# TensorE's loop waits on one semaphore per engine, takes its counts off behind output projections, and transposed x stays in SBUF for the second 16 heads

## Chip, cores, metric

One core of one Trainium2 chip. The metric is the device time of the whole program in microseconds, the median of several runs. Time before: 792.89 us (3 runs, 792.17 to 793.03).

## The reference

Two independent attention blocks, A and B, joined along the last axis. Each has its own x, key cache, value cache and weights, all bf16.

```python
B, Sq, D = 16, 64, 640;  H, Sk, Dh = 32, 512, 128
q = (x @ wq).reshape(B, Sq, H, Dh).transpose(0, 2, 1, 3)
scores = einsum("bhqd,bhkd->bhqk", q, k_cache) * (Dh ** -0.5)
p = softmax(scores)
o = einsum("bhqk,bhkd->bhqd", p, v_cache)
out = o.transpose(0, 2, 1, 3).reshape(B, Sq, H * Dh) @ wo
```

Keys and values are 268 MB of the 298 MB that move. They are read once. The inputs are small, so the scores are close to zero and the softmax is nearly flat.

## The kernel before

The work is cut into 128 *slots* (four heads of one pair of batches) and four *quarters* of 32 slots (16 heads of one block). Each engine has a program of operations sorted by planned time. A slot on TensorE: scores S, transposes of normalized probabilities TR (two halves), output projection OP of an earlier slot, query projection QP of the next slot, weighted sum PV of the slot before. Every fourth slot also transposes x (XT). The other engines and the DMA queue are fully unrolled; TensorE runs a loop of four slots. Its waits must then have the same counts in every turn, so at the end of each turn TensorE subtracts from each semaphore what the turn has consumed.

```python
own = {"XE", "QE", "KT", "NM", "TE", "OE", "OA", "OV", "LDV", "LDX"}   # waited for by TensorE
...
return (("q_" if for_pe(op) else "s_") + op.kind.lower(),)   # one semaphore per kind of operation
...
lo = next(i for i, o in enumerate(pe) if o.kind == "S" and o.idx == cfg.FIRST)   # FIRST = 3, PERIOD = 4
...
for op in prog[:lo]:
    emit(e, op, p, {})
with e.Fori(0, reps):                                        # L720; reps = 31
    for op in prog[lo:lo + size]:
        emit(e, op, p, {})
    for s, v in sorted(per.items(), key=str):
        e.sem_inc(sems[p][s], -v * units(s))                 # L724: the subtractions
```

Loads are issued by SyncE in one fixed order, into rings: 7 slots of K, 4 slots of V, 4 pieces of query weights. Each quarter has 5.2 MB of weights of its own.

```python
# K: rows of 4096 bytes; V: rows of 2048; query weights: rows of 1024; output weights and x: rows of 1280
src = blocks[...][3].rearrange("(kt p) n -> p kt n", p=128)[:, :, c * 512:(c + 1) * 512]
ins = e.dma_start(ws_ring[:, op.idx % NWS], src)             # query weights, four pieces a quarter
...
ins = e.dma_start(xn_ring[:, op.idx % NXN, :], src)          # x, loaded again in every quarter
```

## Time and profile before

| | before |
|---|---|
| time, median | 792.89 us |
| span of the profiled run | 790.7 us |
| TensorE busy | 706.0 us (89%) |
| bytes moved | 297.8 MB |
| starts of S in one turn of the loop | 5.70, 5.41, 5.41, 6.77 us apart |

First the page of the kernel before: TensorE's busy time; then, over 40 equal slices, DMA's busy share in tenths and its rate; the packets; and the engines' shares of the chain that ended last.

```profile
PE 706.0 (89%) x17953; PEld 533.3 (67%) x18081; DVE 616.3 (78%) x1062; ACT 406.8 (51%) x1185; POOL 386.8 (49%) x550
...
DMA  9999999999999999999999999999999999999950
GB/s 319 388 396 397 396 393 396 393 394 384 396 385 397 391 377 393 390 388 370 382 392 393 398 397 397 398 396 390 383 389 387 396 399 397 400 398 399 399 215 15
DMA packets 132396, 297.76 MB, mean 377 GB/s; under 512 B 9472, under 2 KB 34048, under 8 KB 132352
...
PE 60%; PEld 14%; issue 10%; DVE 8%; SPq 4%; DMA 1%; PEldq 1%; ACT 0%; DVEq 0%
```

DMA is at nine tenths or more for almost the whole run, yet the chain is TensorE's: 60% matmuls, 14% weight loads, 10% issue. Two limits lie close together.

TensorE's instructions in order of time around one turn's end (start, duration, engine, line, operation, count, and in brackets the idle time before and what ended it):

```profile
396.83 0.89 PE L622 MATMUL ps<-pT_ring,v_ring 64*128 64x64 bf16 x50
397.66 0.62 PE L604 MATMUL ps<-ident,pn_ring 128*128 128x128 bf16 x8
399.58 0.68 PE L562 MATMUL ps<-kt_ring,qs_ring 32*64 32x512 bf16 x16 [1.30 <-PEq L724]
```

The transposes end at 398.28; S starts at 399.58, after 1.30 us. The line of the subtractions, with what waited for it (us in all, times):

```profile
L724 PEldq EVENT_SEMAPHORE  x372: 51/51/51, 71.2 to 771.8; - x186
...
  PE ps L562: 39.9, 31
```

In the trace they are 12 a turn, 151 ns apart, followed by an add (36 ns) and a compare-and-branch (208 ns): 2.17 us of TensorE's sequencer, from 397.38 to 399.58. About 0.87 us of it lies under the weighted sum and the transposes, which went on meanwhile; 1.30 us shows, 31 times.

The issuing queue's longest wait (us in all, times, longest):

```profile
SPq L508 <- PE ps L622: 243.3, 91, 4.5
```

SyncE waits for V buffers that PV (L622) frees. Last, busy time by stretches of 23.3 us: busy us and (count) of five engines, granted clock, DMA share, GB/s.

```profile
core 0: us, PE busy (x) PEld busy (x) DVE busy (x) ACT busy (x) POOL busy (x), PEclk, DMA share, GB/s
...
263.10:286.40 23.30, 21.78 (x564) 16.51 (x567) 19.13 (x35) 12.65 (x38) 10.85 (x17) 1.00 1.03 377
...
356.34:379.60 23.26, 21.74 (x564) 16.47 (x566) 19.11 (x34) 12.61 (x38) 10.85 (x16) 1.00 1.02 367
...
566.13:589.40 23.27, 21.78 (x564) 16.49 (x567) 19.18 (x34) 12.66 (x39) 18.04 (x23) 1.00 1.05 387
589.44:612.70 23.26, 21.77 (x565) 16.48 (x567) 19.17 (x34) 12.65 (x39) 13.21 (x19) 1.00 1.05 387
612.75:636.10 23.35, 21.83 (x565) 16.55 (x567) 19.28 (x34) 12.70 (x39) 10.91 (x17) 1.00 1.04 399
```

DMA's rate is 367 to 399 GB/s. (A DMA share over 1, here 1.02 to 1.05, means that the packets' times overlap a little.)

### The profile page before, as it was taken

The numbers are of one execution on the slowest core, as the hardware profiler recorded it, in microseconds if no ns is written. First come the engines' busy times: TensorE is split into PE (matmuls) and PEld (weight loads), VectorE is DVE, ScalarE is ACT, GpSimd is POOL, SyncE is SP. The second block draws the span as 40 slices with busy tenths as digits, with TensorE's granted clock in tenths as the row PEclk, the third lists the DMA queues.
The fourth block names the chain that finished last, engine by engine and source line by source line (L and its number), as shares of the span: only waits on it lengthen the run. The fifth ranks groups of instructions, "written<-read, shape, count | busy, mean of one in ns | idle before, by whom it ended". The sixth has DMA issues, their size and how long they took to land.

```text
span 790.7 us, 40216 instructions
## 1 busy us (share of the span) xinstructions
PE 706.0 (89%) x17953; PEld 533.3 (67%) x18081; DVE 616.3 (78%) x1062; ACT 406.8 (51%) x1185; POOL 386.8 (49%) x550
## 2 busy tenths in 40 slices
PE   4668999999999999999999999999999999999994
PEld 3446676776777767767776676767767777677672
DVE  3537888778888788788878888887888887888883
ACT  2334555555546555555555555555555555555551
POOL 5323454444864444445674444444484544444451
PEclk9879999999999999999999999999999999999999
DMA  9999999999999999999999999999999999999950
GB/s 319 388 396 397 396 393 396 393 394 384 396 385 397 391 377 393 390 388 370 382 392 393 398 397 397 398 396 390 383 389 387 396 399 397 400 398 399 399 215 15
DMA packets 132396, 297.76 MB, mean 377 GB/s; under 512 B 9472, under 2 KB 34048, under 8 KB 132352
## 3 DMA queue, kind: packets, MB, share of 16 engines
q1 hardware_dynamic: 130048, 294.69, 98.9%
q10 hardware_dynamic: 2304, 2.62, 0.9%
q8 instruction: 11, 0.18, 0.1%
q14 instruction: 33, 0.27, 0.1%
HBM read 294.65 MB, written 2.62 MB: 376 GB/s over the span
## 4 chain that ended last, share of the span: by engine, by line
PE 60%; PEld 14%; issue 10%; DVE 8%; SPq 4%; DMA 1%; PEldq 1%; ACT 0%; DVEq 0%
PE ps L562 13%; PE ps L604 12%; PE ps L539 11%; PE ps L622 11%; PE ps L638 8%; PE ps L641 5%; PEld ps L539 5%; PEld ps L622 4%; PEld ps L604 3%; DVE pT_ring L610 3%; SPq L501 2%; DVE kt_ring L552 2%; PE ps L522 2%; DMA xn_ring<-in_A_x_dram 1%; PEld ps L638 1%
## 5 line engine op out<-in xcount | busy, mean ns | idle before, releaser
L597 POOL TENSOR_SCALAR pn_ring<-p_ring,recip 128x512 bf16<-128x512 bf16 x512 | 347.7, 692 | 383.1 <-DVE recip L592 382.1
L577 ACT ACTIVATE p_ring<-ps 128x512 bf16<-128x512 f32 x512 | 298.9, 599 | 189.2 <-PE ps L562 189.2
L552 DVE STREAM_TRANSPOSE kt_ring<-kn_ring 128x1024 f32<-128x1024 f32 x256 | 316.4, 1236 | 16.1 <-DMA kn_ring<-in_A_k_cache_dram 15.8
L610 DVE COPY pT_ring<-ps 128x1024 bf16<-128x1024 bf16 x256 | 173.2, 677 | 118.4 <-PE ps L604 117.8
L562 PE MATMUL ps<-kt_ring,qs_ring 32*64 32x512 bf16 x4096 | 147.1, 398 | 46.5 <-PEq L724 39.9
L539 PE MATMUL ps<-xT_ring,wqp_sb 128*128 128x128 bf16 x2560 | 166.3, 221 | 2.4 <-POOL wqp_sb L516 1.3
L539 PEld LDWEIGHTS ps<-xT_ring,wqp_sb 128*128 128x128 bf16 x2560 | 152.5, 114 | 18.7 <-ACT p_ring L577 2.2
L629 ACT ACTIVATE oT_ring<-ps 128x512 bf16<-128x512 f32 x128 | 76.4, 597 | 170.5 <-PE ps L622 170.5
L604 PE MATMUL ps<-ident,pn_ring 128*128 128x128 bf16 x2048 | 159.8, 221 | 1.3 <-DVE pT_ring L610 1.3
L604 PEld LDWEIGHTS ps<-ident,pn_ring 128*128 128x128 bf16 x2048 | 117.3, 98 | 50.5 <-DVE pT_ring L610 42.6
L622 PE MATMUL ps<-pT_ring,v_ring 64*128 64x64 bf16 x8192 | 142.3, 190 | 2.9 <-issue 2.2
L622 PEld LDWEIGHTS ps<-pT_ring,v_ring 64*128 64x128 bf16 x8192 | 126.8, 95 | 15.1 <-issue 2.5
L641 PE MATMUL ps<-wo_sb,oT_ring 128*128 128x128 bf16 x512 | 112.5, 220 | 8.0 <-ACT oT_ring L629 0.9
L638 PE MATMUL ps<-wo_sb,oT_ring 128*128 128x512 bf16 x384 | 118.8, 381 | 0.0
L562 PEld LDWEIGHTS ps<-kt_ring,qs_ring 32*64 32x64 bf16 x4096 | 54.8, 104 | 88.9 <-PEq L724 45.3
L577 ACT ACTIVATION_READ_ACCUMULATOR p_ring<-ps 128x1 f32 x512 | 106.9, 209 | 0.0
L545 DVE TENSOR_SCALAR qs_ring<-ps 128x512 bf16<-128x512 f32 x128 | 85.3, 667 | 0.5 <-PE ps L539 0.5
L638 PEld LDWEIGHTS ps<-wo_sb,oT_ring 128*128 128x128 bf16 x512 | 50.4, 98 | 46.7 <-issue 1.1
L641 PEld LDWEIGHTS ps<-wo_sb,oT_ring 128*128 128x128 bf16 x512 | 50.4, 98 | 0.0
L592 DVE RECIPROCAL recip<-rowsum 128x2 f32<-128x2 f32 x256 | 37.0, 144 | 13.7 <-ACT p_ring L577 13.5
L651 DVE TENSOR_TENSOR acc<-acc,ps 128x128 f32<-128x128 f32 x96 | 27.0, 281 | 10.9 <-PE ps L641 2.1
L528 ACT ACTIVATE xT_ring<-ps 128x640 bf16<-128x640 bf16 x32 | 22.3, 696 | 15.0 <-PE ps L522 15.0
(23 smaller groups left out, 99.7 us busy)
## 6 DMA issues: line engine op xcount, KB each, us to landing
kn_ring<-in_A_k_cache_dram SPq DMA_DIRECT2D x128, 512.0 KB, 9.3
v_ring<-in_A_v_cache_dram SPq DMA_DIRECT2D x128, 512.0 KB, 7.5
kn_ring<-in_B_k_cache_dram SPq DMA_DIRECT2D x128, 512.0 KB, 12.3
v_ring<-in_B_v_cache_dram SPq DMA_DIRECT2D x128, 512.0 KB, 10.5
ws_ring<-in_A_wq_dram SPq DMA_DIRECT2D x8, 640.0 KB, 10.0
wo_sb<-in_A_wo_dram SPq DMA_DIRECT2D x8, 640.0 KB, 10.1
ws_ring<-in_B_wq_dram SPq DMA_DIRECT2D x8, 640.0 KB, 10.4
wo_sb<-in_B_wo_dram SPq DMA_DIRECT2D x8, 640.0 KB, 12.3
```

What stands on the lines that cost most here:

```text
L539: last = e.matmul(ps[:, 0, f * 128:(f + 1) * 128], w[:, kt, f, :], xT_ring[:, xs, kt, :], start=(kt == 0), stop=(kt == KT - 1))
L545: ins = e.tensor_scalar(qs_ring[:, op.idx % NQ].rearrange("p f b q -> p (f b q)"), ps[:, 0, :], scale, None, ALU.mult)
L552: ins = e.transpose(dst, kn_ring[:, n % NK, b, :].bitcast(F32))
L562: last = e.matmul(ps[64 * b:64 * b + 64, i, :], qs_ring[rows, n % NQ, f, b, :], kt_ring[rows, n % NKT, b, :, f // 2, :, f % 2], start=(f = ...
L577: ins = e.activation(dst, src, ACTF.Exp, scale=1.0, accum_out=rowsum[:, h:h + 1])
L597: ins = e.tensor_scalar(pn_ring[:, (h // 2) % NPN, :, h % 2, :], p_ring[:, (h // 2) % NP, :, h % 2, :], recip[:, (h // 2) % NR, h % 2:h % ...
L604: last = e.transpose(pt_ps[:, t, :], pn_ring[:, op.idx % NPN, t].rearrange("q s k -> q (s k)"), ident[:, :])
L610: ins = e.tensor_copy(pT_ring[:, op.idx % NT].rearrange("p t q -> p (t q)"), pt_flat)
L622: last = e.matmul(o_ps[:, s, col:col + 64], v_ring[rows, n % NV, b, a, t, :], pT_ring[rows, (2 * n + a) % NT, t, 64 * b:64 * b + 64], star ...
L629: ins = e.activation(oT_ring[:, op.idx % NO].rearrange("p s a q -> p s (a q)"), o_ps, ACTF.Copy)
L638: last = e.matmul(out_ps0, oT, wo_sb[:, 4 * j + h4, 0:N0], start=(j == 0 and h4 == 0), stop=(j == NJ - 1 and h4 == 3))
L641: last = e.matmul(out_ps1, oT, wo_sb[:, 4 * j + h4, N0:D], start=(h4 == 0), stop=(h4 == 3))
```

## The change

Its intent: take TensorE's loop overhead off the critical path, and load x once per block.

- All operations of one engine that TensorE waits for count on one semaphore. Waits on V keep four. 12 subtractions a turn become 7.
- Each subtraction goes behind an output projection after the last wait on its semaphore; the turn is cut before QP, so the branch lies behind a projection too.
- Transposed x is copied by GpSimd into SBUF (XS) in a block's first quarter and read from there in the second. x's landing is awaited by a ScalarE operation before the x transposes, no longer by TensorE itself. The x transposes on TensorE stay (the loop must be periodic); only their result is not used.
- One K buffer less makes room. The planned times change a little.

```diff
-    NK = 7
+    NK = 6
-    FIRST = 3
+    FIRST = 4
...
+        first = dims["FIRST"](g // NBP)
+        add("act", "XE", g, n0 + AT["XE"], [] if first else [("xs", g % NBP)], [("OB",), ("xT", g % cfg.NX)])
+        if first:
+            add("pool", "XS", g, n0 + AT["XS"], [("xT", g % cfg.NX)], [("xs", g % NBP)])
+            op = add("sp", "LDX", g, txt - 0.5, [], [("xn", g % cfg.NXN)])
...
-    lo = next(i for i, o in enumerate(pe) if o.kind == "S" and o.idx == cfg.FIRST)
+    lo = next(i for i, o in enumerate(pe) if o.kind == "QP" and o.idx == cfg.FIRST)
...
-        return (("q_" if for_pe(op) else "s_") + op.kind.lower(),)
+        return ("q_" + op.eng,) if for_pe(op) else ("s_" + op.kind.lower(),)
...
+def place_takes(turn, per):
+    spots = [i for i, o in enumerate(turn) if o.kind == "OP"] + [len(turn) - 1]
+    load = {i: 0 for i in spots}
+    take = {}
+    for s in sorted(per, key=str):
+        final = max(i for i, o in enumerate(turn) for s2, _ in o.waits if s2 == s)
+        best = min((i for i in spots if i >= final), key=lambda i: (load[i] + 2 * (i == len(turn) - 1), i))
+        load[best] += 1
+        take[s] = best
+    return take
...
-                for s, v in sorted(per.items(), key=str):
-                    e.sem_inc(sems[p][s], -v * units(s))
+                    for s, v in sorted(per.items(), key=str):
+                        if loop["take"][s] == i:
+                            e.sem_inc(sems[p][s], -v * units(s))
+                            taken[s] = v
```

More of the change, by code (lines that the diff above doesn't have):

```diff
@@ L31 @@
     PERIOD = 4
-    FIRST = 3
+    FIRST = 4
     SLOT_US = 5.6
-    AT = dict(XT=-0.999, XE=-0.813, QP=-0.735, QE=-0.179, KT=(-0.798, -0.573), S=0, EX=(0.133, 0.239, 0.393, 0.529),
-              RC=(0.25, 0.562), NM=(0.632, 0.647, 0.673, 0.713), TR=(0.953, 1.086), TE=(1.035, 1.243), PV=1.274,
-              OE=1.62, OP=2.212, OA=2.264, OV=2.887, ST=3.562, WP0=-1.75, WP1=-2.894)
+    AT = dict(XT=-0.998, XE=-0.828, XS=1.064, QP=-0.639, QE=-0.339, KT=(-1.008, -0.378), S=0,
+              EX=(0.14, 0.192, 0.454, 0.611), RC=(0.31, 0.63), NM=(0.476, 0.739, 0.793, 0.91), TR=(0.854, 1.001),
+              TE=(0.983, 1.034), PV=1.464, OE=1.653, OP=2.236, OA=2.301, OV=2.96, ST=3.466, WP0=-1.75, WP1=-2.974)
     DMA_US = dict(LDK=1.27, LDV=1.35, LDWQ=1.75, LDWO=1.75, LDX=0.45)
@@ L84, in build_plan @@
         add("pe", "XT", g, txt, [("xn", g % cfg.NXN), ("ident",)], [("OB",)])
-        add("act", "XE", g, n0 + AT["XE"], [], [("OB",), ("xT", g % cfg.NX)])
-        op = add("sp", "LDX", g, txt - 0.5, [], [("xn", g % cfg.NXN)])
-        loads.append((txt - 0.1, (g - cfg.NXN) * NJ + AT["XT"] if g >= cfg.NXN else -99.0, 0, op))
+        first = dims["FIRST"](g // NBP)
[3 more added lines that the diff above has]
+            op = add("sp", "LDX", g, txt - 0.5, [], [("xn", g % cfg.NXN)])
+            loads.append((txt - 0.1, (g - cfg.NXN) * NJ + AT["XT"] if g >= cfg.NXN else -99.0, 0, op))
     for ph in range(NPH):
@@ L189, in build_plan @@
     pe = progs["pe"]
-    lo = next(i for i, o in enumerate(pe) if o.kind == "S" and o.idx == cfg.FIRST)
-    hi = next(i for i, o in enumerate(pe) if o.kind == "S" and o.idx == cfg.FIRST + cfg.PERIOD)
+    lo = next(i for i, o in enumerate(pe) if o.kind == "QP" and o.idx == cfg.FIRST)
+    hi = next(i for i, o in enumerate(pe) if o.kind == "QP" and o.idx == cfg.FIRST + cfg.PERIOD)
     size = hi - lo
@@ L205, in build_plan @@
             op.deps = [d for d in op.deps if d.kind != "LDWO"]
+        if op.kind == "XT" and op.idx > 0:
+            next(d for d in op.deps if d.kind == "OE").deps.extend(d for d in op.deps if d.kind == "LDX")
+            op.deps = [d for d in op.deps if d.kind != "LDX"]
         if op.kind == "QP" and op.idx > 0:
@@ L208, in build_plan @@
             op.deps = [d for d in op.deps if d.kind != "WP"]
-    own = {"XE", "QE", "KT", "NM", "TE", "OE", "OA", "OV", "LDV", "LDX"}
+    own = {"XE", "QE", "KT", "NM", "TE", "OE", "OA", "OV", "LDV"}
     def for_pe(d):
@@ L268, in build_plan @@
     loop["per"] = per
+    loop["take"] = place_takes(progs["pe"][lo:lo + size], per)
     return progs, counts, loop
+def place_takes(turn, per):
[8 more added lines that the diff above has]
+    return take
 def run_order(progs, visit):
@@ L415, in mha_kernel @@
     for general in (False, True):
-        dims = dict(NPH=NPH, NBP=NBP, NJ=NJ, FINAL=lambda ph: ph % NSUB == NSUB - 1)
+        dims = dict(NPH=NPH, NBP=NBP, NJ=NJ, FIRST=lambda ph: ph % NSUB == 0,
+                    FINAL=lambda ph: ph % NSUB == NSUB - 1)
         plans.append(build_plan(dims, cfg, general))
@@ L433, in mha_kernel @@
         xT_ring = sb("xT_ring", [128, NX, KT, 128], BF16)
+        xs_sb = sb("xs_sb", [128, NBP, KT * 128], BF16)
         xn_ring = sb("xn_ring", [128, NXN, D], BF16)
@@ L527, in em_XE, with em_XS @@
         def em_XE(e, op):
-            ins = e.activation(xT_ring[:, op.idx % NX].rearrange("p k q -> p (k q)"), x_ps[:, 0:KT * 128], ACTF.Copy)
+            src = xs_sb[:, op.idx % NBP, :] if op.idx // NBP % NSUB else x_ps[:, 0:KT * 128]
+            ins = e.activation(xT_ring[:, op.idx % NX].rearrange("p k q -> p (k q)"), src, ACTF.Copy)
+            return ins, ins
+        def em_XS(e, op):
+            ins = e.tensor_copy(xs_sb[:, op.idx % NBP, :], xT_ring[:, op.idx % NX].rearrange("p k q -> p (k q)"))
             return ins, ins
@@ L720, in run_program @@
             with e.Fori(0, reps):
-                for op in prog[lo:lo + size]:
-                    emit(e, op, p, {})
-                for s, v in sorted(per.items(), key=str):
-                    e.sem_inc(sems[p][s], -v * units(s))
+                taken = {}
+                for i, op in enumerate(prog[lo:lo + size]):
+                    emit(e, op, p, taken)
+                    for s, v in sorted(per.items(), key=str):
+                        if loop["take"][s] == i:
+                            e.sem_inc(sems[p][s], -v * units(s))
+                            taken[s] = v
             taken = {s: v * reps for s, v in per.items()}
```

## The prediction

> **What bounds the kernel now.** Two almost equal limits, in a loop of 31 turns of four slots (a slot: four heads of two batches).
>
> TensorE: starts of the score matmuls (instructions in time order) are 5.70, 5.41, 5.41 and 6.77 us apart, 23.3 us a turn. 5.41 us is dense matmul work; 5.70 has the x transposes. 6.77 is the turn's end: 12 semaphore subtractions 151 ns apart (1.81 us), then add and branch (0.36 us). They start before the weighted sum's last matmuls and outlast the transposes behind them; the score matmul then idles 1.30 us (waits view: 39.9 us in 31 times).
>
> DMA: 297.8 MB, share 1.03 to 1.05 in nearly every turn (busy time by stretches). The best sustained rate is 398 GB/s (612 to 752 us); it fell to 377 and 367 GB/s in turns where K and V alone come at TensorE's pace and the issuing queue waits for V buffers (243 us in its waits). A quarter (one block's 16 heads) needs 73.7 MB, 185 us at 398 GB/s; TensorE needs 8 x 23.3 = 186 us.
>
> **What the change does.**
> - One semaphore per engine: I count 7 subtractions a turn (three engines, four V buffers), one or two behind each output projection, and the branch behind one too. A projection streams for 1.09 us, so 0.15 to 0.5 us of sequencer time should fit beneath it. [...]the present subtractions start while the weighted sum still runs. I expect turns of 22.0 to 22.3 us, 34 to 40 us less over 31 turns if nothing else bound.
> - x is loaded once per block: 16 loads of 160 KB less, 2.6 MB, 6.6 us at 398 GB/s. The x transposes remain (0.39 us a turn); ScalarE then copies from SBUF instead of PSUM (0.70 us now). GpSimd copies 16 times, estimated 0.7 us each from its 1.25 us for 1280 columns; it is 49% busy.
> - K buffers 7 to 6: harmless once DMA is the limit. The engines' order stays nearly the same.
>
> **How much counts.** TensorE alone would end near 758 us. But it would ask for 9.1 MB per 22.2 us, over 409 GB/s, which the trace never shows; DMA becomes the limit. 295.1 MB at 396 to 398 GB/s, with the slow first 10 us (253 GB/s), lets the last V land at 746 to 750 us (765 now, held back by V buffers). After it come three more weighted sums at TensorE's pace and the end, 17 to 20 us (now 10 us from the last weighted sum). Span 764 to 769, plus 2 us to the measured time. So about 25 of the 34 to 40 us count; the rest becomes waiting for K and V.
>
> **Predicted: 768 us, 759 to 777 (8 in 10).** Chances: faster by over 2% 0.88, within 2% 0.11, slower 0.01.
>
> **What would show it.** No idle time put down to subtractions; no 6.77 us slots; TensorE waiting for K transposes or V instead; DMA at 395 to 399 GB/s in all turns; V-buffer waits of the issuing queue well under 243 us; 295.1 MB; the first 50 us as slow as now (DMA's).
>
> **What would make it wrong.** Subtractions stalling the queue behind the projections after all (then about 780); merged semaphores or the new order creating waits on VectorE (78% busy); DMA over 400 GB/s once more loads are queued (then near 760); six K buffers starving a quarter's start, where 5.2 MB of weights come on top.

## The result, and the profile after

779.62 us (4 runs, 779.26 to 780.16) against 792.66 us: ratio 0.9836, interval 0.9819 to 0.9853, so 1.6% faster. A ratio is the mean time of one kernel's runs over that of the other's of the same rounds, so it is not quite the ratio of the quoted medians. The prediction had 768 us, 759 to 777, and gave 0.88 to a gain of over 2%. It missed on both counts.

The page of the changed kernel:

```profile
PE 708.3 (91%) x17953; PEld 534.6 (69%) x18081; DVE 607.9 (78%) x1062; ACT 412.2 (53%) x1185; POOL 394.6 (51%) x566
...
DMA  8999999999999999999999999999999999999960
GB/s 318 389 395 397 394 396 395 394 396 391 392 387 399 398 400 400 400 394 394 387 389 395 397 397 397 397 397 398 374 387 388 398 398 399 400 398 400 400 254 15
DMA packets 130096, 295.20 MB, mean 380 GB/s; under 512 B 9216, under 2 KB 31744, under 8 KB 130048
...
PE 54%; SPq 27%; DMA 14%; issue 2%; DVE 2%; ACT 0%; DVEq 0%; ACTq 0%
SPq L531 13%; PE ps L567 11%; PE ps L590 11%; SPq L524 11%; PE ps L632 11%; PE ps L650 11%; PE ps L666 7%; DMA kn_ring<-in_B_k_cache_dram 6%; DMA v_ring<-in_A_v_cache_dram 5%; PE ps L669 4%; DMA kn_ring<-in_A_k_cache_dram 2%; SPq L517 2%; D
```

The chain has turned: TensorE's 74% (60% matmuls and 14% weight loads) are 54%, its issue went from 10% to 2%, and 41% are now the DMA queue and landings (SPq 27%, DMA 14%). TensorE at a turn's end, in a stretch that nothing holds:

```profile
481.38 0.62 PE L632 MATMUL ps<-ident,pn_ring 128*128 128x128 bf16 x8
481.84 0.44 PE L545 MATMUL ps<-ident,xn_ring 128*128 128x128 bf16 x5
...
483.15 0.22 PE L669 MATMUL ps<-wo_sb,oT_ring 128*128 128x128 bf16 x1
483.20 1.28 PE L567 MATMUL ps<-xT_ring,wqp_sb 128*128 128x128 bf16 x20
```

No line has idle time in brackets: transposes, x transposes, projection and QP follow each other. The subtractions' line, now L754, has nobody waiting for it (no line follows "who waited" in this view):

```profile
L754 PEldq EVENT_SEMAPHORE  x210: 51/51/51, 53.6 to 735.4; - x105
...
who waited for it (us, times):
```

7 a turn, in 30 turns. The trace has the last four and the branch from 481.58 to 482.49, while TensorE works on transposes and projection until 483.2. The issuing queue's wait for V buffers fell from 243.3 us to:

```profile
SPq L531 <- PE ps L650: 48.8, 30, 3.8
```

What TensorE waits for instead is K (its transposes on VectorE, and the scaled q that VectorE can only give after them):

```profile
DVE kt_ring L580 <- DMA kn_ring<-in_B_k_cache_dram: 24.6, 16, 3.6
PE ps L590 <- DVE qs_ring L573: 23.7, 15, 3.2
DVE kt_ring L580 <- DMA kn_ring<-in_A_k_cache_dram: 16.1, 5, 7.3
```

The same stretches as before:

```profile
263.10:286.40 23.30, 23.09 (x617) 17.68 (x621) 20.16 (x36) 13.51 (x38) 12.14 (x19) 1.00 1.04 399
...
356.34:379.60 23.26, 21.80 (x564) 16.49 (x566) 18.82 (x34) 12.86 (x38) 15.49 (x21) 1.00 1.05 388
...
566.13:589.40 23.27, 18.85 (x506) 14.40 (x506) 14.28 (x25) 10.40 (x31) 14.29 (x18) 1.00 1.05 388
589.44:612.70 23.26, 16.84 (x424) 12.46 (x425) 15.70 (x28) 10.00 (x29) 8.22 (x13) 1.00 1.04 393
612.75:636.10 23.35, 22.72 (x593) 16.98 (x597) 20.25 (x36) 12.91 (x37) 12.02 (x18) 1.00 1.04 399
```

In the first one TensorE is busy for 23.09 of 23.30 us. Around the start of the last quarter (566 to 613 us) it is busy for 18.85 and 16.84 us, and the third quarter's start looks alike (20.52 and 17.95 us in two such stretches from 380 to 426 us), although DMA's share is full (1.04 and 1.05 in all four). TensorE got its time back and waits there for data.

Starts of S, and the end of the span, show where the time went (worked out from the starts in the traces, us):

```
                S4     S104    S127    end    | S4 to S104  S104 to end
before         53.1   638.1   772.2   790.7  |   585.1        152.6
changed        52.5   629.7   758.2   777.3  |   577.2        147.6
```

Up to S4 nothing changed, as predicted. In the 100 slots from S4 to S104 the change gained 7.9 us, after them 5.0 us. Slots that nothing holds take 5.69, 5.41, 5.42, 5.41 us, so a turn is 21.93 us, 1.4 us less than before; over 31 turns that would have been 42 us.

One more thing differs at the very end. TensorE stalls without any wait in the slots after its loop (a third, shorter one is not shown):

```profile
740.44 0.56 PE L632 MATMUL ps<-ident,pn_ring 128*128 128x128 bf16 x7
741.73 0.23 PE L632 MATMUL ps<-ident,pn_ring 128*128 128x128 bf16 x1 [0.73 <-issue]
...
745.69 1.10 PE L590 MATMUL ps<-kt_ring,qs_ring 32*64 32x512 bf16 x26
747.66 0.43 PE L590 MATMUL ps<-kt_ring,qs_ring 32*64 32x512 bf16 x6 [0.86 <-issue]
```

### The profile page after: what moved, and what is told of

Its sections match the earlier page's. It is cut to its first block, busy times and chain, and to the rows that moved or that the text cites. A ratio compares the mean times of both kernels' runs of the same rounds, so it can differ in the third digit from the quotient of the medians.

```text
span 777.3 us, 40034 instructions
## 1 busy us (share of the span) xinstructions
PE 708.3 (91%) x17953; PEld 534.6 (69%) x18081; DVE 607.9 (78%) x1062; ACT 412.2 (53%) x1185; POOL 394.6 (51%) x566
## 4 chain that ended last, share of the span: by engine, by line
PE 54%; SPq 27%; DMA 14%; issue 2%; DVE 2%; ACT 0%; DVEq 0%; ACTq 0%
SPq L531 13%; PE ps L567 11%; PE ps L590 11%; SPq L524 11%; PE ps L632 11%; PE ps L650 11%; PE ps L666 7%; DMA kn_ring<-in_B_k_cache_dram 6%; DMA v_ring<-in_A_v_cache_dram 5%; PE ps L669 4%; DMA kn_ring<-in_A_k_cache_dram 2%; SPq L517 2%; DMA xn_ring<-in_A_x_dram 1%; DVE kt_ring L580 1%; PE ps L545 1%
## 5 line engine op out<-in xcount | busy, mean ns | idle before, releaser
L567 PEld LDWEIGHTS ps<-xT_ring,wqp_sb 128*128 128x128 bf16 x2560 | 153.0, 114 | 18.8 <-ACT p_ring L605 2.2
L632 PEld LDWEIGHTS ps<-ident,pn_ring 128*128 128x128 bf16 x2048 | 115.7, 98 | 65.8 <-DVE pT_ring L638 51.2
L605 ACT ACTIVATION_READ_ACCUMULATOR p_ring<-ps 128x1 f32 x512 | 105.1, 205 | 0.0
L545 PE MATMUL ps<-ident,xn_ring 128*128 128x128 bf16 x160 | 15.0, 227 | 16.5 <-ACT oT_ring L657 10.4
```

The costliest lines, as they stand in the source:

```text
L567: last = e.matmul(ps[:, 0, f * 128:(f + 1) * 128], w[:, kt, f, :], xT_ring[:, xs, kt, :], start=(kt == 0), stop=(kt == KT - 1))
L605: ins = e.activation(dst, src, ACTF.Exp, scale=1.0, accum_out=rowsum[:, h:h + 1])
L632: last = e.transpose(pt_ps[:, t, :], pn_ring[:, op.idx % NPN, t].rearrange("q s k -> q (s k)"), ident[:, :])
```

## The experiments

The kernel before ran beside each group of runs, at 792.07 to 792.50 us, so medians of different groups can be set side by side; ratios are to the kernel before of the same rounds.

### 1 and 2. Both kernels with half of V left out: before_light, after_light

```diff
+            dst = v_ring[:, n % NV, b].rearrange("p a t d -> p a (t d)")
+            if n >= NV:
+                src, dst = src[:, 0:1], dst[:, 0:1]
-            ins = e.dma_start(v_ring[:, n % NV, b].rearrange("p a t d -> p a (t d)"), src)
+            ins = e.dma_start(dst, src)
```

The results are wrong (relative error 0.93). One run each, so their state is unknown; their granted clocks, 0.986 and 0.988, are those of the fast runs.

> The kernel before with half of every V load left out after the first four slots (wrong result on purpose; 65 MB less, so DMA should not bind). If the kernel before was held by TensorE's loop as read from its trace (turns of 23.3 us), it hardly gets faster: 780 to 790 us, slots of 5.7, 5.4, 5.4 and 6.76 us. If DMA had been its limit it would fall below 760 us.

> The changed kernel with the same half of V left out (wrong result on purpose). My theory (TensorE's turn is really 21.9 us and only DMA hides it): slots 5.7, 5.4, 5.4, 5.4 us from start to end, no long slots at the starts of the quarters, 740 to 750 us, about 40 us under the light kernel before. Rival (the changed order or the merged semaphores make TensorE wait on other engines at the starts of the quarters): the long slots at 60 to 68 and 93 to 103 stay and it ends near 770 us.

before_light: 792.49 us, the time of the kernel before, with 65 MB less to load. Its wait for the subtractions (us, times, longest) is unchanged too:

```profile
PE ps L565 <- PEq L727: 39.9, 31, 1.3
```

after_light: 751.19 us, and every slot from S8 on within 5.41 to 5.70 us. TensorE from 100 to 700 us, first the changed kernel, then after_light (columns as above: PE busy first, rate last):

```profile
100.00:700.00 600.00, 572.60 (x14667) 434.06 (x14772) 494.50 (x865) 336.32 (x970) 318.84 (x455) 0.99 1.04 395
```

```profile
100.00:700.00 600.00, 599.87 (x15427) 451.47 (x15426) 514.40 (x904) 352.15 (x1016) 331.23 (x474) 1.00 0.91 317
```

599.87 of 600 us busy, against 572.60 us in the changed kernel. So, after the start (the first four slots' V is whole in all of them), the kernel before was held by TensorE, the change is worth 41.3 us to TensorE (792.49 - 751.19), and loading the whole of V takes 28.4 us of that back (779.62 - 751.19). The rival, waits brought in by the new order, falls: the order is the same in after_light.

### 3. x in SBUF alone: x_only

The kernel before with six K buffers, the XS copy and one load of x per block; its semaphores, its subtractions at the end of the turn and its order stay. (x's landing is awaited by an operation of ScalarE, as in the change, so that the loop is periodic; that makes 11 subtractions.)

> x kept in SBUF and six K buffers, but the semaphores, the subtractions and the order of the kernel before. If DMA was not yet the limit before, 2.6 MB less gains little: 788 to 793 us, turns still 23.2 us. If DMA was the limit, it gains 6.6 us: 786 us.

789.87 us, ratio 0.9971 (0.9957 to 0.9985): 2.3 us gained. The long slots fell from 6.76 to 6.64 us, one subtraction less; 31 x 0.12 = 3.7 us covers the gain, and no saving of DMA time is needed for it. (The profiled span fell by 4.0 us, from 790.6 to 786.6 us in the mean of the runs. Time outside the span, which each run lists as the difference of the two, rose from 1.7 to 3.3 us.) As long as TensorE was the limit, the 2.6 MB were worth nothing that could be seen.

### 4. The loop alone: takes_nk6

The changed kernel without XS: x is loaded in every quarter again.

```diff
-        dims = dict(NPH=NPH, NBP=NBP, NJ=NJ, FIRST=lambda ph: ph % NSUB == 0,
+        dims = dict(NPH=NPH, NBP=NBP, NJ=NJ, FIRST=lambda ph: True,
...
-            src = xs_sb[:, op.idx % NBP, :] if op.idx // NBP % NSUB else x_ps[:, 0:KT * 128]
+            src = x_ps[:, 0:KT * 128]
```

> The changed kernel, but x is loaded again for the second 16 heads (2.6 MB more). If the changed kernel is held by DMA, that costs the transfers' time: 16 x 160 KB in packets of 1280 bytes, 6.6 to 7.2 us, 786 to 787 us. If it is held by anything else (waits on other engines, too few K buffers), it costs 0 to 3 us.

784.85 us, ratio 0.9902: 5.2 us above the changed kernel by the ratios (0.9902 - 0.9836, of 792.5). A little under the expected 6.6 to 7.2 us, far over 0 to 3. By the spans it is 6.1 us (783.2 against 777.1 us, means): without XS the time outside the span is 1.7 us, as before the change, with it 2.6 us. The same saving is worth 5 us here and next to nothing in run 3: what a byte is worth depends on which limit holds.

### 5. Fewer query weights: wq_cut

```diff
+            dst = ws_ring[:, op.idx % NWS]
+            if op.idx >= NWS:
+                src, dst = src[:, 0:1], dst[:, 0:1]
-            ins = e.dma_start(ws_ring[:, op.idx % NWS], src)
+            ins = e.dma_start(dst, src)
```

> The changed kernel, but the query weights of quarters 2 to 4 are loaded only to a fifth (wrong result on purpose; 6.3 MB less in packets of 1 KB). If DMA's time is the limit and these packets move at the 341 GB/s that their 48 ns in the trace give, it gains 17 to 18 us: about 762 us, and the long slots at the starts of the quarters shrink. At 398 GB/s it would gain 15.8 us. If the long slots come from the order or the waits of the change, it gains under 3 us.

761.71 us, ratio 0.9622: 17.9 us under the changed kernel's 779.62 (17.0 by the ratios). The long slots shrank: S4 to S104 took 559.0 us instead of 577.2, 18.2 us less. The 6144 packets left out, at 48 ns (their median in the trace of the changed kernel) on 16 engines, are an estimated 18.4 us. So the long slots are DMA time. The arithmetic is wrong (four fifths of the query weights are the first quarter's), yet the comparison passed: the flat softmax hides it. "Correct" therefore says little about the query weights in the runs below; wq_wide's index arithmetic puts the same column of the same row in the same place, which is argued, not shown by the comparison.

### 6. One K buffer less: after_nk5

`NK = 6` becomes `NK = 5`.

> The changed kernel with five K buffers instead of six. My theory (DMA is busy all the time, and buffers only set how much is loaded ahead): 0 to 2 us more. Rival (the step from seven to six K buffers, which came with the change, is what starves TensorE at the starts of the quarters): a further step costs 5 us or more, 785 us or over.

779.5 us, ratio 0.9844 (0.9829 to 0.9859), the same as the changed kernel. A further step down costs nothing, so the step from seven to six is unlikely to be what starves TensorE; the changed kernel with seven was not run.

### 7 and 8. The same weights earlier, and in longer rows: wq_early, wq_wide

wq_early queues the query weights of quarters 2 to 4 before the first of them is needed:

```diff
-            add("pool", "WP", w, twp, [("ws", w % cfg.NWS)], [("wqp", j)])
-            op = add("sp", "LDWQ", w, twp - 0.5, [], [("ws", w % cfg.NWS)])
+            add("pool", "WP", w, twp, [("ws", i) for i in range(NJ)] if ph else [("ws", j)], [("wqp", j)])
+            tld = ph * PH + AT["WP1"] - 0.3 - 0.75 * (NJ - 1 - j) if ph else twp - 0.3
+            op = add("sp", "LDWQ", w, tld - 0.2, [], [("ws", w % cfg.NWS)])
...
```

wq_wide does the same, and cuts the weights by blocks of the contraction instead of by columns, so that one row of the source is 4096 bytes:

```diff
-            ins = e.dma_start(ws_ring[:, op.idx % NWS], src)
+            if op.idx < NJ:
+                ins = e.dma_start(ws_ring[:, :, j * 512:(j + 1) * 512], src[:, :, c * 512:(c + 1) * 512])
+            else:
+                k0, k1, n0 = j, j + 1 if j < NJ - 1 else KT, c // NJ * NJ * 512
+                ins = e.dma_start(ws_ring[:, k0:k1, :], src[:, k0:k1, n0:n0 + NJ * 512])
...
```

(Left out: the ring's shape, and GpSimd's copies, which read the new layout.)

> The changed kernel with the query weights of quarters 2 to 4 queued earlier, all four before the first is rearranged. The same bytes in the same packets, only earlier: if DMA's total time is the limit, within 2 us of the changed kernel; if it is the crowding at the starts of the quarters, 3 us or more faster.

> As wq_early, but the query weights of quarters 2 to 4 come in rows of 4096 bytes (five blocks of rows by the contraction, all columns of the quarter) instead of 1024 bytes. The same bytes. If small packets are what lowers the rate at the starts of the quarters: from 7680 packets of 48 ns to 1920 of 164 ns on 16 engines, 3 us faster than wq_early, about 776 us, and 395 GB/s or more where there were 367 to 376. If the rate fell for another reason, no gain.

wq_early: 780.43 us, ratio 0.9854, no gain. wq_wide: 776.79 us, ratio 0.9813 (0.9800 to 0.9827): 3.2 us faster than wq_early (0.9854 - 0.9813, of 792.1), as expected from the packets. Busy time by stretches before the fourth quarter, first wq_early, then wq_wide; the last column is GB/s:

```profile
520.00:543.00 23.00, 22.74 (x573) 17.26 (x577) 19.89 (x35) 13.81 (x40) 11.43 (x17) 1.00 1.01 371
543.00:566.00 23.00, 19.29 (x510) 14.77 (x511) 14.62 (x27) 11.14 (x34) 12.22 (x17) 1.00 1.05 388
566.00:589.00 23.00, 21.26 (x528) 15.87 (x525) 19.00 (x33) 12.81 (x37) 17.74 (x23) 1.00 1.04 393
```

```profile
520.00:543.00 23.00, 22.79 (x612) 17.49 (x615) 19.66 (x34) 13.07 (x39) 12.49 (x19) 1.00 1.04 399
543.00:566.00 23.00, 18.34 (x492) 13.74 (x494) 15.56 (x29) 10.36 (x29) 12.66 (x18) 1.00 1.04 399
566.00:589.00 23.00, 22.12 (x577) 16.58 (x565) 19.25 (x34) 12.80 (x37) 18.10 (x23) 1.00 1.03 383
```

While query weights come (the first two stretches) the rate is 399 instead of 371 and 388 GB/s. From 566 to 612 us come output weights in rows of 1280 bytes, 2048 packets in both kernels. There wq_wide has only 383 GB/s in both stretches of 23 us, but wq_early 393 and 392. So the deepest dip went with the 1 KB rows, while a part of the loss moved into the next stretches. Row lengths do not explain that part, and no run shows what does.

### 9 to 11. Which part of the loop's change matters: merged_only, kinds_behind, cut_at_s

merged_only keeps the merging, but cuts the turn before S and puts all 7 subtractions at its end. kinds_behind keeps the moving, but has one semaphore per kind again. cut_at_s has both, but the turn is cut before S.

```diff
 merged_only, beside the lines of cut_at_s:
-        best = min((i for i in spots if i >= final), key=lambda i: (load[i] + 2 * (i == len(turn) - 1), i))
+        best = len(turn) - 1
 kinds_behind:
-        return ("q_" + op.eng,) if for_pe(op) else ("s_" + op.kind.lower(),)
+        return (("q_" if for_pe(op) else "s_") + op.kind.lower(),)
 cut_at_s:
-    FIRST = 4
+    FIRST = 3
...
-    lo = next(i for i, o in enumerate(pe) if o.kind == "QP" and o.idx == cfg.FIRST)
+    lo = next(i for i, o in enumerate(pe) if o.kind == "S" and o.idx == cfg.FIRST)
...
```

> The changed kernel with its turn cut before the score matmul again, as before, and all subtractions at the turn's end: only the merging of the semaphores is left. Of the 2.17 us of 12 subtractions and branch before, 1.30 us showed, so 0.87 us was hidden; 7 subtractions and the branch are 1.42 us, of which 0.5 to 0.6 us should show: long slots of 5.95 us in the stretches where DMA does not hold TensorE. In time little: that is 17 us of TensorE's, most of it out of the 31 us that TensorE waits for DMA anyway: 780 to 785 us.

> The changed kernel with one semaphore per kind of operation again (11 or so subtractions), placed behind the output projections by the same rule: only the moving is left. The sequencer is 1.5 us ahead there, so even three subtractions in one place are hidden: slots of 5.41 and 5.69 us as in the changed kernel and the same time, 779 to 781 us. If the merging mattered for the waits, slots get longer.

> The changed kernel with the turn cut before the score matmul: merged, moved where possible, but four subtractions or so and the branch (0.96 us) remain at the old place. 0.87 us fit there, so 0.1 us shows per turn: slots of 5.5 us, time 779 to 781 us.

merged_only: 782.28 us, ratio 0.9878; long slots of 6.12 to 6.15 us, so 0.7 us show instead of the expected 0.5 to 0.6. They are in the waits again (18.8 us in 29 times):

```profile
PE ps L590 <- PEq L754: 18.8, 29, 0.7
```

kinds_behind: 781.06 us, ratio 0.987; all slots that DMA does not hold are 5.41 and 5.69 us. Moving alone hides the subtractions in the slots; merging is not needed for it. The time is 1.4 us over the changed kernel's by the medians and 2.7 us by the ratios (one of the four runs took 783.07 us); 0.8 us of it lies outside the span (3.4 against 2.6 us). cut_at_s: 778.89 us, ratio 0.9834; slots of 5.66 to 5.70 us where the branch is, 0.26 us instead of the expected 0.1. It is nevertheless not slower than the changed kernel: it has only one slot after its loop, and not the stalls of the changed kernel there, which led to run 13.

### 12. Less TensorE work: pe_light

```diff
-            for h4 in range(4):
+            for h4 in (0, 3):
```

Wrong (relative error 0.70).

> The changed kernel with half of the output projections' matmuls left out (wrong result on purpose): 0.54 us less TensorE work per slot, 69 us in all, and the same DMA. If DMA alone set the changed kernel's time, it stays within 2 us of 779.6 us. My theory now (DMA holds TensorE at the starts of the quarters, but from the start of the last quarter to the end TensorE is the limit again, so that V buffers hold the last loads): the last V lands near 751 us instead of 756 and the end comes within 18 us of it, 768 to 773 us.

775.51 us, ratio 0.9798: 4 us less for 69 us less TensorE work. Neither expectation was met: the last V landed at 756.3 us, just as in the changed kernel, and S4 to S104 took 578.0 us (577.2 in the changed kernel). So V buffers do not hold the last loads; that part of my theory is wrong. Until S104 DMA's time is the limit, not TensorE's work. What the lighter kernel gains comes after S104 (143.2 instead of 147.6 us).

The traces also show how the last V is late. The times at which the pieces of the last slot's V landed (two loads, 16 engines, so 32 pieces; from the trace's semaphore events, us):

```
changed      first 748.1   28 of the 32 by 751.2   the last four: 754.0 755.1 755.2 756.3
pe_light     first 748.3   28 of the 32 by 751.3   the last four: 753.9 754.8 755.2 756.3
after_light  first 719.8   all 32 by 720.9
```

Four pieces are 3 to 5 us behind the others, which fits two of the 16 engines (the trace does not name them). The loads of K, whose pieces can be told apart load by load, show the same: from 612 to 740 us in the changed kernel 14 of the 16 pieces land within 1.6 us of the first, the last two after 5.1 and 6.4 us (medians). The distance had grown over the run, in which DMA's share was 1.04 from 10 to 740 us: from first to last piece it was 2.6 us between 60 and 170 us. In before_light and after_light it is 1.5 and 2.1 us at the end. The program waits for a load's last piece: its waits count 16 pieces a load. What makes these pieces fall behind, no run shows.

### 13 to 15. The last slots: first3, wide_first3, wide_first3_fl

first3 is the changed kernel with `FIRST = 3`: 31 turns fit, and one slot instead of four runs after the loop. wide_first3 adds this to wq_wide. wide_first3_fl also moves VectorE's check of the row sums, and with it the two small operations that follow from it (FLM, FLC; left out here):

```diff
-        add("dve", "FL1", 0, N - 1 + AT["RC"][1] + 0.002, [("rs", h) for h in range(4 * N)], [("good",)])
...
+        add("dve", "FL1", 0, N - 1 + AT["TE"][1] + 0.01, [("rs", h) for h in range(4 * N)], [("good",)])
...
```

> The changed kernel with its loop begun one slot earlier, so that 31 turns fit instead of 30 and one slot, not four, runs after the loop. If the stalls of the last slots are the fetching of instructions after the loop, slots of 6.3, 6.7 and 5.8 us become 5.4 to 5.7 and the time falls by 2 to 2.5 us, to about 777 us. If TensorE waits for K or V there, nothing changes.

> wq_wide with the loop begun one slot earlier. DMA ends 3 us earlier and the end is 2 us shorter; the two add up if TensorE's last slots follow DMA: 774 to 775 us. If they are the same 3 us seen twice, 776 us.

> As wide_first3, with VectorE's check of the row sums moved behind the last copy of transposed probabilities. The copy waits about 1.3 us for it now: 773 us, 1 to 1.5 us less than wide_first3.

first3: 777.29 us, ratio 0.982 (0.9807 to 0.9833): 2.3 us less. The last slots are 5.41 us; the S that was torn in two in the changed kernel is whole:

```profile
744.75 1.14 PE L590 MATMUL ps<-kt_ring,qs_ring 32*64 32x512 bf16 x32
745.82 0.62 PE L632 MATMUL ps<-ident,pn_ring 128*128 128x128 bf16 x8
```

The 16 KB packets of one DMA queue that brings instructions (q8 in the page) agree. In the changed kernel seven of them come before 74 us, then none until 739.3, 745.2, 750.7 and so on; in first3 the first one after the loop comes at 754.6. So in the changed kernel they came until the loop's first turn ended (its branch ran at 73.1 us), none in the other 29 turns, and again behind the last branch (735.6 us): what follows the loop is fetched. That these packets are TensorE's is read from their times alone. A full DMA seems to be part of the stall: in after_light, with the same program but DMA's share at 0.39 where the loop ends (712 to 720 us; 1.01 from 740 to 750 us in the changed kernel), TensorE has none of these stalls, and the last slots take 5.65, 5.42 and 5.42 us (one run).

wide_first3: 773.95 us, ratio 0.9772 (0.9759 to 0.9786), 2.3% faster than the kernel before and the best of all. The two gains add up.

wide_first3_fl: 774.95 us, ratio 0.9788, a miss. VectorE in order of time at its end:

```profile
758.82 0.69 DVE L646 COPY pT_ring<-ps 128x1024 bf16<-128x1024 bf16 x1 [0.72 <-PE ps L640]
759.42 0.68 DVE L708 TENSOR_REDUCE extreme<-rowsum 128x1 f32<-128x512 f32 x1
...
760.98 0.17 DVE L715 TENSOR_TENSOR good<-extreme 128x1 bf16<-128x1 f32 x1
761.05 0.28 DVE L687 TENSOR_TENSOR acc<-acc,ps 128x128 f32<-128x128 f32 x1
```

The copy came earlier, but the row sums' check (L708 to L715) now stands before the addition of a projection's result (L687), and the last weighted sum waits for that one: 1.6 us idle. Moving the check took one wait away and made another.

## Why the prediction was wrong

Right, point by point:

- *TensorE held the kernel before*: before_light, 792.49 us with 65 MB less.
- *The subtractions and the branch fit beneath the projections*: turns of 21.93 us (predicted 22.0 to 22.3), no wait left for them, and TensorE's gain is 41 us (predicted 34 to 40), both a little better than forecast. The trace shows that TensorE's work goes on meanwhile: the last four subtractions and the branch run from 481.58 to 482.49 us, while TensorE works on transposes and projection until the QP behind them starts at 483.20 us, 1.6 us after the first of the four. kinds_behind and merged_only add that behind the projections the number does not matter; at the turn's end it does (0.7 us show of 7, 1.30 us of 12).
- *DMA then becomes the limit, and the rest turns into waiting for K and V*: runs 2, 4, 5 and 12. *Six K buffers are harmless*: after_nk5.

Wrong: the size of DMA's time. Of TensorE's 41 us only 13 counted, where the prediction had about 25 of 34 to 40. It put "the last V land at 746 to 750 us" and "the end, 17 to 20 us" after it; it was 756.3 and 21.0 us (777.3 - 756.3), 11 us over the middle of the two. Three terms, and a small one outside this sum:

1. *"295.1 MB at 396 to 398 GB/s"* took the best stretch's rate for all bytes. The rate was 394.6 GB/s from 10 to 740 us. The prediction's own sign, "DMA at 395 to 399 GB/s in all turns", failed: the three turns from 543 to 613 us had 376, 388 and 393. At 397 that is 4.4 us less ((397 - 394.6) / 397 x 730, an estimate). Packets of 1024, 1280, 2048 and 4096 bytes take 48, 55, 87 and 164 ns in the trace (medians, changed kernel from 30 us on), which is 341, 372, 377 and 400 GB/s on 16 engines. Packets overlap a little (DMA's share is 1.04), so the real rates are an estimated 4% higher. A straight line through these four durations leaves an estimated 10 ns that do not depend on the size. wq_wide got 3.2 us back with the same bytes. I had not weighed the row lengths. A part of the dips is not explained by them (experiments 7 and 8). The dips to 387 GB/s at the starts of quarters were in the trace before; I took them all for TensorE's pace.
2. *The last landing.* 28 of 32 pieces had landed by 751.2 us, the last at 756.3. The prediction counted bytes and not the slowest pieces: 5 us. That the lag costs the whole run as much is argued from pe_light, where DMA is the limit and ends equally late; no run took the lag away.
3. *The end after the last V.* The changed loop leaves four slots behind it where the kernel before left one, and TensorE stalls there while packets of instructions come again (0.73 and 0.86 us of idle time in two of the slots): 2.3 us (first3). Without it the end comes 18.1 us after the last V (774.5 - 756.4), inside the predicted 17 to 20.
4. *"plus 2 us to the measured time"*: time outside the span is 2.6 us, against 1.7 us before. All runs with XS have 2.4 us or more, takes_nk6 without it 1.7. This is 0.6 us of the miss; what costs the time there, no run shows.

The first three make 12 us for 11; the terms overlap a little, since the late pieces' lag is also part of the rate. The mechanism was right; the step that failed is the sum for DMA's time: its rate (394.6 instead of 396 to 398 GB/s), its last landing (756.3 instead of 746 to 750 us) and the tail after it (21.0 instead of 17 to 20 us). Because the forecast was built from a best rate and a smallest tail, every error went the same way. I had also set the chance of a gain over 2% by the middle of that sum and not by its one-sidedness.

## What to carry to other kernels

Where two limits lie within 2% of each other, removing one is worth only the distance to the other (here 13 of 41 us): make the second one light (half of its bytes, wrong results and all) to see both sizes before and after. For DMA's time, sum the packets by their row length with durations from the trace (here 48 ns for 1 KB, 164 ns for 4 KB) and allow for the pieces that land last (here 5 us); do not multiply all bytes by the best rate. Bookkeeping in a loop is best put behind instructions that keep the engine busy (here 7 subtractions and the branch showed 0.7 us a turn at the turn's end, and nothing behind the projections), and a loop should run to the end of the work, as what followed it here cost 2.3 us.
